# Weights of an MLP moved to another address phase against the moving operand

## The chip, the cores and the metric

The kernel runs on one core of a Trainium2 chip. The metric is the time of one execution on the device in microseconds; lower is better. Each core has a matrix engine (TensorE, PE in the profile, with its weight loads listed apart as PEld), VectorE (DVE), ScalarE (ACT), GpSimd (POOL) and a DMA queue driven by SyncE (SP). Operands lie in SBUF, an on-chip memory of 128 partitions; matrix products are written to PSUM.

A matrix product on TensorE has two operands in SBUF. The weights (128 x 128 here) are loaded into the array by an instruction of their own, and then the moving operand (128 partitions by up to 512 columns) passes through the array.

## The reference

Eight batches of eight heads, 576 positions, head dimension 64. Heads 0 to 3 attend to the last 32 positions, heads 4 to 7 to the positions with the same remainder modulo 32. The attention's output, put back to 512 features a position, goes through a gated MLP with 1,024 hidden features:

```
scores = q @ k.T / 8, masked; attn = softmax(scores); x = attn @ v
h    = maximum(x @ w_in, 0)
conv = conv_w[0]*h[t-1] + conv_w[1]*h[t] + conv_w[2]*h[t+1]
out  = (h * sigmoid(conv)) @ w_out
```

All inputs are 32-bit floats; the kernel gets the weights as pairs of 32-bit words of 64-bit numbers and converts them itself.

## The kernel before, in words

The 4,608 positions are cut into nine groups of 512 (N). For each group the kernel computes four attention steps (one for each pair of heads) of the next batch, the first product of the MLP (`mm1`, L607), the convolution, sigmoid and gate on ScalarE, VectorE and GpSimd (`conv_gate`), and the second product (`mm2`, L672).

Both products are done with split numbers, so that 32-bit accuracy comes out of the faster 32-bit matrix format: every operand is a high part and a low part, and three products are added up: high weights by high moving part, low weights by high moving part, high weights by low moving part. The weights are `wih`, `wil` (first product) and `woh`, `wol` (second); the moving operands are `xh`, `xl` (attention's output, two groups' worth of columns) and `gh`, `gl` (the gated hidden features, one row of 512 columns for each of eight feature blocks; 514 in the last group). Each single matmul has its own weight load of 128 x 128 and, as a rule, 512 moving columns. One block of the first product is 4 x 3 matmuls, one block of the second 8 x 3. The last group's second product is cut into pieces of 256 and 257 columns (258 with the one that is computed twice).

At the beginning the weights are converted (`convert`, L334 to L421): words are loaded into `ws` or `misc`, cut into parts on ScalarE and VectorE, and the low parts are formed by matmuls with the unit matrices `eye`, `eyer` and `negr` (minus one) as weights (L411 to L413, L418, L419).

The order of the instructions on each engine comes from a planner: each operation is entered with an estimated duration and a due time, the planner lays them out, and the program is emitted in that order. The planner knows engines, durations and dependencies; addresses do not enter it.

The tiles in SBUF are allocated from the pools `const` and `mlp`, one after the other in the order in which they are declared, so the order of the declarations sets the addresses. A tile's bytes per partition are the product of its later dimensions and the element size: `xh`, `xl`, `wih`, `wil`, `woh` and `wol` have 16,384 bytes each, `gh` and `gl` 16,448, `diag` 1,280, `eye`, `eyer`, `negr` and `warm` 512, `cwords` 192, `picks` and `small` 128, `cwa` and `cwt` 96, `carry` 64. The declarations stand from L268 on.

Of the kernel before, what the change touches and what calls it, by code (L numbers as in the profile page):

```python
# [10 lines left out]
F32 = _mybir.dt.float32  # L11
F32R = _mybir.dt.float32r
BF16 = _mybir.dt.bfloat16
I32 = _mybir.dt.int32
# [6 lines left out]
P = 128  # L21
W = 32
# [227 lines left out]
def tile_banded_attention_gated_mlp(ctx, tc, qkT, vw, w_in, conv, w_out, masks_in, picks_in, eye_in, out):  # L250
# [3 lines left out]
    D, NSEG, NBLK = 64, 4, 5  # L254
    SEGS = [0, 5, 9, 14, 18]
    NF, NM = w_in.shape[0], w_out.shape[0] // 2
# [11 lines left out]
    const = ctx.enter_context(tc.tile_pool(name="const", bufs=1))  # L268
    xh = const.tile([P, NC, 2 * N], F32R, name="xh")
    xl = const.tile([P, NC, 2 * N], F32R, name="xl")  # L270
    wih = const.tile([P, NC, FF], F32R, name="wih")
    wil = const.tile([P, NC, FF], F32R, name="wil")
    woh = const.tile([P, NF, DM], F32R, name="woh")
    wol = const.tile([P, NF, DM], F32R, name="wol")
    gh = const.tile([P, NF * (N + 2)], F32R, name="gh")
    eye = const.tile([P, P], F32, name="eye")
    eyer = const.tile([P, P], F32R, name="eyer")
    negr = const.tile([P, P], F32R, name="negr")
    picks = const.tile([P, 2, W], BF16, name="picks")
    small = const.tile([P, W], F32, name="small")  # L280
    cwords = const.tile([P, 3 * NF, 2], I32, name="cwords")
    gl = const.tile([P, NF * (N + 2)], F32R, name="gl")

    def attention_buffers(pool, i):
# [10 lines left out]
    mlp = ctx.enter_context(tc.tile_pool(name="mlp", bufs=1))  # L295
# [2 lines left out]
    misc = mlp.tile([P, 2 * NHB * L], F32, name="misc")  # L298
    hs = [misc[:, L * i:L * i + L] for i in range(NHB)]
    cs = [misc[:, L * (NHB + i):L * (NHB + i) + L] for i in range(NHB)]  # L300
    carry = mlp.tile([P, NF, 2], F32, name="carry")
    psum = ctx.enter_context(tc.tile_pool(name="psum", bufs=1, space=PSUM))
    psR = psum.tile([P, 2048], F32, name="r")
    psM = [psum.tile([P, 512], F32, name=f"m{i}") for i in range(NPM)]
# [1 line left out]
    words = [const.tile([P, 8 * P, 2], I32, name=f"ws{i}") for i in range(NWS)]  # L306
    wa = [const.tile([P, 8 * P], I32, name=f"wa{i}") for i in range(NWA)]
    wl = [const.tile([P, 8 * P], F32R, name=f"wl{i}") for i in range(NWL)]
    diag = const.tile([P, 2 * NBLK, W], F32, name="diag")
    cwa = const.tile([P, 3 * NF], I32, name="cwa")  # L310
    cwt = const.tile([P, 3 * NF], I32, name="cwt")

    def slot(n):
        return n % NB
# [368 lines left out]
        if g == NG - 1 and not last:  # L683
            op(Q, 256, at + 6, lambda: nc.sync.dma_start(out=out[ms, first:first + N + 1], in_=o[:, 0:N + 1]), ko, [])

    warm_ = const.tile([P, 256], BF16, name="warm")

    def warm_up():
        nc.vector.memset(warm_, 0.0)
# [113 lines left out]
```

## Time and profile before

| | |
|---|---|
| time, median of 3 runs | 532.12 us (531.75 to 533.3) |
| profiled execution, its own time | 531.87 us |
| its span, first to last instruction | 529.7 us |
| granted TensorE clock, mean | 0.986 |
| busy: TensorE, weight loads, VectorE, ScalarE, GpSimd | 508.4, 409.9, 362.3, 319.8, 118.3 us |
| matmuls of the first product (L607) | 3 x 288 |
| matmuls of the second product (L672) | 3 x 320, of these 3 x 256 with 512 columns |

The profile is of one execution. Matmuls overlap in it: a matmul's listed duration runs from its start to its modelled end, and the next one starts before that, so durations do not add up to the span. Weight loads (PEld) run beside the matmul that stands before them. The granted clock is the share of full speed that TensorE's throttle allowed. "Lnnn" is a line of the kernel.

### The profile page before, as it was taken

What the parts mean: (1) busy time and instruction counts of PE and PEld (TensorE: products, weight loads), DVE (VectorE), ACT (ScalarE), POOL (GpSimd) and SP (SyncE); (2) the same over time, 40 slices, a digit from 0 to 9 for tenths busy, and PEclk for the clock granted to TensorE, in tenths of its full rate; (3) what the DMA queues carried; (4) which work ended last, traced back from release to release, by engine and by line L of the source; (5) the groups of instructions that cost most, each with busy time, mean ns of one, the idle gap of its engine ahead of it and who ended that gap; (6) DMA issues with size and microseconds to landing.
All of it is one profiled execution on the core that took longest, in us unless ns stands there. A gap on an engine that the chain in (4) does not pass through costs nothing.

```text
span 529.7 us, 16633 instructions
## 1 busy us (share of the span) xinstructions
PE 508.4 (96%) x7352; PEld 409.9 (77%) x7352; DVE 362.3 (68%) x639; ACT 319.8 (60%) x492; POOL 118.3 (22%) x197
## 2 busy tenths in 40 slices
PE   4787999999999999999999999999999999999997
PEld 3555677778877887788778877887788788888897
DVE  3977799866785668757975785688658845832940
ACT  2454776856584668656837675577547755733841
POOL 0111201532222112212231222222212221320220
PEclk9797999999999999999999999999999999999999
DMA  8656422352044303520334034303440001001001
GB/s 281 250 189 222 157 78 78 124 178 88 7 136 149 99 1 127 185 76 23 114 107 147 1 124 145 121 0 119 135 134 1 33 11 72 1 16 65 0 36 44
DMA packets 17639, 51.30 MB, mean 97 GB/s; under 512 B 2208, under 2 KB 3360, under 8 KB 17568
## 3 DMA queue, kind: packets, MB, share of 16 engines
q1 hardware_dynamic: 17568, 50.25, 28.1%
q8 instruction: 57, 0.93, 0.7%
q14 instruction: 14, 0.11, 0.1%
HBM read 40.80 MB, written 9.44 MB: 95 GB/s over the span
## 4 chain that ended last, share of the span: by engine, by line
PE 93%; ACT 2%; DVE 2%; DMA 1%; issue 1%; SPq 1%; DVEq 0%; ACTq 0%
PE m L672 39%; PE m L607 37%; PE r L514 6%; PE r L458 4%; PE m L411 2%; PE r L449 1%; DMA misc<-in_dram 1%; PE r L569 1%; PE m L412 0%; PE m L413 0%; ACT xh L549 0%; PE r L486 0%; DVE t L471 0%; DVE mx L470 0%; ACT wa L334 0%
## 5 line engine op out<-in xcount | busy, mean ns | idle before, releaser
L643 DVE SCALAR_TENSOR_TENSOR misc<-misc,cw 128x512 f32<-128x512 f32 (+29 forms) x256 | 126.8, 542 | 35.5 <-ACT misc L634 35.0
L672 PE MATMUL m<-gh,woh 128*128 128x512 f32 (+2 forms) x320 | 123.7, 387 | 0.0
L672 PE MATMUL m<-gh,wol 128*128 128x512 f32 (+2 forms) x320 | 118.2, 370 | 0.0
L672 PE MATMUL m<-gl,woh 128*128 128x512 f32 (+2 forms) x320 | 117.9, 368 | 0.0
L607 PE MATMUL m<-xh,wih 128*128 128x512 f32 x288 | 113.3, 393 | 0.0
L607 PE MATMUL m<-xh,wil 128*128 128x512 f32 x288 | 112.5, 391 | 0.0
L607 PE MATMUL m<-xl,wih 128*128 128x512 f32 x288 | 112.3, 390 | 0.0
L492 POOL TENSOR_TENSOR t<-t,sm 128x640 f32<-128x640 f32 x31 | 45.3, 1462 | 117.6 <-DVE sm L476 82.9
L672 PEld LDWEIGHTS m<-gh,woh 128*128 128x128 f32 x320 | 60.0, 188 | 12.2
L624 ACT ACTIVATE misc<-m 128x512 f32<-128x512 f32 x72 | 42.9, 596 | 42.8 <-PE m L607 41.0
L672 PEld LDWEIGHTS m<-gl,woh 128*128 128x128 f32 x320 | 60.2, 188 | 10.8
L672 PEld LDWEIGHTS m<-gh,wol 128*128 128x128 f32 x320 | 60.2, 188 | 8.4
L607 PEld LDWEIGHTS m<-xh,wih 128*128 128x128 f32 x288 | 54.2, 188 | 11.8 <-issue 0.2
L607 PEld LDWEIGHTS m<-xl,wih 128*128 128x128 f32 x288 | 54.2, 188 | 11.5
L607 PEld LDWEIGHTS m<-xh,wil 128*128 128x128 f32 x288 | 54.2, 188 | 11.0
L648 DVE TENSOR_TENSOR misc<-misc 128x512 f32<-128x512 f32 (+1 forms) x69 | 48.8, 708 | 12.6 <-ACT misc L646 12.4
L634 ACT ACTIVATE misc<-misc,cw 128x512 f32<-128x512 f32 (+1 forms) x70 | 50.5, 724 | 11.1 <-DVE gl L434 4.7
L646 ACT ACTIVATE misc<-misc 128x512 f32<-128x512 f32 (+1 forms) x72 | 44.6, 627 | 14.5 <-DVE misc L643 13.8
L431 ACT CAST gh<-misc 128x512 fp32r<-128x512 f32 (+1 forms) x72 | 44.2, 618 | 14.0 <-DVE misc L648 12.3
L678 ACT COPY misc<-m 128x512 f32<-128x512 f32 (+2 forms) x40 | 21.5, 545 | 47.5 <-PE m L672 47.0
L626 POOL COPY misc<-carry 128x2 f32<-128x2 f32 x64 | 18.9, 295 | 131.2 <-DVE misc L648 95.9
L470 DVE TENSOR_REDUCE mx<-r 128x10 f32<-128x640 f32 x32 | 26.2, 819 | 30.4 <-PE r L458 30.4
(84 smaller groups left out, 584.0 us busy)
## 6 DMA issues: line engine op xcount, KB each, us to landing
qk<-in_dram SPq DMA_DIRECT2D x32, 592.0 KB, 4.0
v<-in_dram SPq DMA_DIRECT2D x32, 384.0 KB, 3.6
ws<-in_dram SPq DMA_DIRECT2D x14, 512.0 KB, 5.1
out_dram<-misc SPq DMA_DIRECT2D x28, 256.0 KB, 3.1
misc<-in_dram SPq DMA_DIRECT2D x2, 512.0 KB, 6.3
out_dram<-misc SPq DMA_DIRECT2D x4, 255.5 KB, 3.4
out_dram<-misc SPq DMA_DIRECT2D x3, 256.5 KB, 2.0
masks<-in_dram SPq DMA_DIRECT2D x2, 160.0 KB, 2.6
```

Source lines behind the costliest of these rows:

```text
L431: op(A, ta, at, lambda: nc.scalar.copy(hi(), src), [skey], [(k, "h") for k in [key] + over])
L470: op(V, 0.826, at + offset[0], lambda: nc.vector.tensor_reduce(out=mx, in_=p3, axis=AX.X, op=ALU.max), ks, [("mx", i)])
L492: op(G, 1.28, at + offset[5], lambda: nc.gpsimd.tensor_tensor(out=t, in0=t, in1=sm.unsqueeze(2).to_broadcast([P, 2 * NBLK, 64]), op=ALU.mu ...
L514: nc.tensor.matmul(psV[64 * h:64 * h + 64, o:o + n_], v[W * c:W * c + W, h, j], tt[W * c:W * c + W, 64 * NBLK * h + a:64 * NBLK * h + z], ...
L607: nc.tensor.matmul(ps, a[:, c, fs], x[:, c, N * x0:N * x0 + N], start=(n == 0 and m == 0), stop=(n == NC - 1 and m == 2))
L624: op(A, 0.596, at + cg[2], lambda: nc.scalar.activation(out=h[:, 2:N + 2], in_=ps, func=AF.Relu), [kp], [("h", hi)])
L634: op(A, 0.725, at + cg[3], lambda: nc.scalar.activation(out=c_[:, :n], in_=h[:, 1:n + 1], func=AF.Copy, scale=w1), kh + ["cw"], [kc] + new)
L643: op(V, 0.11 + 0.00117 * (z - a), at + cg[4] + 0.4 * k, lambda k=k, wk=wk, a=a, z=z: nc.vector.scalar_tensor_tensor(out=c_[:, a:z], in0=h[ ...
L646: op(A, 0.63, at + cg[5], lambda: nc.scalar.activation(out=c_[:, :n], in_=c_[:, :n], func=AF.Sigmoid), [kc], [kc], table=1)
L648: op(ge, 0.69 if ge == V else 1.28, at + cg[6], lambda: (nc.vector if ge == V else nc.gpsimd).tensor_tensor(out=c_[:, :n], in0=h[:, 1:n + ...
L672: nc.tensor.matmul(ps, a[:, f, ms], row(y, g, f)[:, tok], start=(f == 0 and n == 0), stop=(f == NF - 1 and n == 2))
L678: op(A, 0.59 if z - a0 == N else 0.38, at + 3 * t + 3, lambda ps=ps, a0=a0, z=z: nc.scalar.copy(o[:, a0:z], ps), [("M", mi)], ko)
```

## The change

Only the order of declarations changes. `cwords` moves ahead of the weights; `diag`, `eye` and `carry` come to stand between the weights and `gh`; `warm`, `cwa` and `cwt` come to stand between `gh` and `gl`. `carry` moves from the pool `mlp` to `const`. No operation, dependency or due time is touched.

```diff
     xh = const.tile([P, NC, 2 * N], F32R, name="xh")
     xl = const.tile([P, NC, 2 * N], F32R, name="xl")
+    cwords = const.tile([P, 3 * NF, 2], I32, name="cwords")
     wih = const.tile([P, NC, FF], F32R, name="wih")
     wil = const.tile([P, NC, FF], F32R, name="wil")
     woh = const.tile([P, NF, DM], F32R, name="woh")
     wol = const.tile([P, NF, DM], F32R, name="wol")
+    diag = const.tile([P, 2 * NBLK, W], F32, name="diag")
+    eye = const.tile([P, P], F32, name="eye")
+    carry = const.tile([P, NF, 2], F32, name="carry")
     gh = const.tile([P, NF * (N + 2)], F32R, name="gh")
-    eye = const.tile([P, P], F32, name="eye")
     eyer = const.tile([P, P], F32R, name="eyer")
     negr = const.tile([P, P], F32R, name="negr")
     picks = const.tile([P, 2, W], BF16, name="picks")
     small = const.tile([P, W], F32, name="small")
-    cwords = const.tile([P, 3 * NF, 2], I32, name="cwords")
+    warm_ = const.tile([P, 256], BF16, name="warm")
+    cwa = const.tile([P, 3 * NF], I32, name="cwa")
+    cwt = const.tile([P, 3 * NF], I32, name="cwt")
     gl = const.tile([P, NF * (N + 2)], F32R, name="gl")
...
-    carry = mlp.tile([P, NF, 2], F32, name="carry")
...
-    diag = const.tile([P, 2 * NBLK, W], F32, name="diag")
-    cwa = const.tile([P, 3 * NF], I32, name="cwa")
-    cwt = const.tile([P, 3 * NF], I32, name="cwt")
...
-    warm_ = const.tile([P, 256], BF16, name="warm")
```

## The prediction

> **What bounds the kernel now.** I read the page first: busy time, the slices, the chain of waits by line, then the costliest groups.
>
> ```profile
> span 529.7 us, 16633 instructions
> PE 508.4 (96%) x7352; PEld 409.9 (77%) x7352; DVE 362.3 (68%) x639; ACT 319.8 (60%) x492; POOL 118.3 (22%) x197
> ...
> PEclk9797999999999999999999999999999999999999
> ...
> PE 93%; ACT 2%; DVE 2%; DMA 1%; issue 1%; SPq 1%; DVEq 0%; ACTq 0%
> PE m L672 39%; PE m L607 37%; PE r L514 6%; PE r L458 4%; PE m L411 2%; PE r L449 1%; DMA misc<-in_dram 1%; PE r L569 1%; PE m L412 0%; PE m L413 0%; ACT xh L549 0%; PE r L486 0%; DVE t L471 0%; DVE mx L470 0%; ACT wa L334 0%
> ```
>
> TensorE is busy for 96% of the span and makes 93% of the chain; the two MLP products, L607 (first) and L672 (second), make 76% of the chain. No other engine is above 68%. The view by stretches says where TensorE is not the bound:
>
> ```profile
> core 0: us, PE busy (x) PEld busy (x) DVE busy (x) ACT busy (x) POOL busy (x), PEclk, DMA share, GB/s
> 0.00:50.00 50.00, 33.26 (x898) 24.68 (x898) 34.73 (x55) 20.85 (x27) 6.84 (x12) 0.87 0.68 239
> ...
> 85.00:480.00 395.00, 395.00 (x5873) 318.23 (x5872) 275.55 (x516) 252.50 (x391) 100.33 (x171) 1.00 0.26 87
> ```
>
> Only in the first 50 us does TensorE idle much (33.26 of 50). From 85 to 480 us it never stops, at a granted clock of 1.00, while VectorE is busy for 275.55 of 395 us, 70%. So from 85 us on the time is the sum of TensorE's start-to-start distances, and I read those next. "Busy" for one matmul (390 ns) is longer than its distance to the next, since matmuls overlap; the distance is what counts. The chain of waits in order of time (start, length, what) gives it from long unbroken runs:
>
> ```profile
> 280.58 21.80 PE m L607 x96
> ...
> 336.11 13.19 PE m L607 x57
> ...
> 462.46 19.04 PE m L672 x84
> 481.50 21.76 PE m L607 x96
> 503.26 22.89 PE m L672 x192
> ```
>
> 21.76 / 96 = **226.7 ns** for each matmul of 128x512 in the first product; 19.04 / 84 = 226.7 in the second. The run at 336 us comes right after an attention step: 13.19 / 57 = 231.4. The last group is cut into 256 and 258 columns (257 in the mean): 22.89 / 192 = 119.2.
>
> What would it be without any hindrance? At half clock the trace has the answer:
>
> ```profile
> 49.35:51.06 1.71, 1.71 (x5) 0.50 0.50 196
> ```
> ```profile
> 50.63 0.61 PE L413 MATMUL m<-wih,negr 128*128 128x512 f32 x1
> 51.06 1.08 PE L411 MATMUL m<-ws,eye 128*128 128x512 f32 x2
> ```
>
> At clock 0.50 a 512-column matmul is followed by the next after 0.43 us, so the columns themselves take about 0.43 / 2 = 0.215 us at full clock, with the rounding of these starts 0.21 to 0.22. A second row is the short bf16 warm-up at full clock, whose length grows with each matmul that the window lets in:
>
> ```profile
> 32.11 0.34 PE L523 MATMUL r<-warm 128*128 128x192 bf16 x2
> ...
> 32.11 0.42 PE L523 MATMUL r<-warm 128*128 128x192 bf16 x3
> ...
> 32.11 0.50 PE L523 MATMUL r<-warm 128*128 128x192 bf16 x4
> ```
>
> 0.08 us for 192 columns is 0.417 ns a column; 512 such columns are 213.3 ns. So every f32 matmul of the MLP takes **13.4 ns more** than its columns. What runs beside it is the next weight load:
>
> ```profile
> 336.38 0.40 PE L607 MATMUL m<-xh,wil 128*128 128x512 f32 x1
> 336.62 0.40 PE L607 MATMUL m<-xl,wih 128*128 128x512 f32 x1
> 336.86 0.40 PE L607 MATMUL m<-xh,wih 128*128 128x512 f32 x1
> 337.09 0.40 PE L607 MATMUL m<-xh,wil 128*128 128x512 f32 x1
> 337.32 0.39 PE L607 MATMUL m<-xl,wih 128*128 128x512 f32 x1
> 337.55 0.39 PE L607 MATMUL m<-xh,wih 128*128 128x512 f32 x1
> 337.78 0.40 PE L607 MATMUL m<-xh,wil 128*128 128x512 f32 x1
> 338.02 0.39 PE L607 MATMUL m<-xl,wih 128*128 128x512 f32 x1
> ```
> ```profile
> 336.38 0.19 PEld L607 LDWEIGHTS m<-xl,wih 128*128 128x128 f32 x1
> 336.62 0.19 PEld L607 LDWEIGHTS m<-xh,wih 128*128 128x128 f32 x1
> ```
>
> Each load starts with the matmul ahead of its own (336.38 and 336.38). After the interruption the distances are 0.24, 0.24, 0.23, 0.23, 0.23, 0.23, 0.24 us and settle at 226.7 later. The same instructions on the same addresses thus take different times: the surplus is not one fixed step of the instruction. It fits two reads of SBUF, moving operand and weights, that get in each other's way depending on how they lie in time. That is my reading, not a thing the trace names.
>
> **The change, part by part.** No instruction, wait or DMA is added, removed or moved: the planner's costs hold no address. What moves is addresses. In bytes per partition, modulo 512, measured from xh: before, xh, xl and the four weight tiles are 16,384 each, so all start at 0, and so does gh; gh's surplus of 64 and picks, small and cwords (128 + 128 + 192) make 512, so gl is at 0 too. A weight block is 128 f32, 512 bytes, and a moving row of the first eight groups 2,048. After, cwords (192) lies ahead of the weights: they start at 192. diag, eye and carry (1,280 + 512 + 64) fill up to 2,048, so gh is at 0, and eyer, negr, picks, small, warm, cwa and cwt (1,984) with gh's 64 bring gl to 0 again. So the change is one thing: the weights' phase against the moving operand goes from 0 to 192.
>
> How many matmuls feel it: L607 864, L672 768 of 512 columns (the groups list them), together **1,632**, and the last group's 192 halves.
>
> ```profile
> L607 PE MATMUL m<-xh,wih 128*128 128x512 f32 x288 | 113.3, 393 | 0.0
> L607 PE MATMUL m<-xh,wil 128*128 128x512 f32 x288 | 112.5, 391 | 0.0
> L607 PE MATMUL m<-xl,wih 128*128 128x512 f32 x288 | 112.3, 390 | 0.0
> L672 PE MATMUL m<-gh,woh 128*128 128x512 f32 x256 | 105.7, 413 | 0.0
> ```
>
> The phase's price at 192 is shown nowhere in the trace, so I bound it. Best: the surplus goes, 226.7 to 213.3 ns, 1,632 x 13.4 = 21.9 us. Worst: the matmuls never settle and stay at the mean after an interruption, 231.4: 1,632 x 4.7 = 7.7 us lost. The surplus changes with small shifts in time, and a shift of addresses shifts the same two reads against each other, so I hold a change of the surplus likelier than none. I take **half of it away**, 6.7 ns: there is no row that is nearer to one end, since the settled 226.7 lies inside the range that the rows show and nothing shows a complete escape. Of the 1,632 the first group's 96 run between 47 and 82 us among weight conversions, on loads that TensorE waits for; I count them at nothing (0.6 us if that cover is gone). 1,536 x 6.7 = **10.3 us**.
>
> The last group has a floor of its own. Weight loads alone, in the trace's low-part matmuls of 2 to 144 columns, follow each other thus:
>
> ```profile
> 42.44 0.86 PEld L569 LDWEIGHTS r<-xh,negr 128*128 128x128 f32 x7 [0.85 <-ACT xh L549]
> ```
>
> (0.86 - 0.19) / 6 = 0.112 us, so 119.2 can fall to 112 at most: 192 x 7.2 = 1.4 us; I take half, **0.7 us**, bounds 0 to 1.4.
>
> The rest has one answer, nothing: eye as weights now at 448 instead of 64 (24 matmuls of L411, 10 ns each is 0.2 us either way), diag used once, warm, cwa, cwt and carry read by engines that are not the bound; attention's tiles move by 2,048, phase unchanged; the f32 tiles of ScalarE and VectorE in misc by 64, hidden under TensorE's 395 of 395 us. Without that cover the whole would cost what those engines lose, and they have 119 us of slack there.
>
> Sum: 10.3 + 0.7 = 11.0 us. The profiled execution took 531.87 (span 529.7 and 2.2 around it), so 520.9; the median of the runs is 0.25 above it, so **521 us**.
>
> The Trainium skill, TensorE: Matmul & The Clock Gate (section "Wait — 56ns, not 53.3ns?"), gives warm back-to-back matmuls N / 2.4 GHz plus about 2.5 ns, 215.7 at 512 columns. The trace's 226.7 is not that. By the page's figure as the floor, the best case would be 1,632 x 11.0, about 18 us (an estimate from that page).
>
> **The rivals.** *Nothing changes* (532). Moving operand and weights don't meet in SBUF, or they meet as often at each phase: the load reads 512 bytes while the moving operand passes more than that, so every phase may be crossed. For it speak the matmuls of the weight conversion, where the phase is already another (eyer and negr at 64, the moving wl at 288):
>
> ```profile
> 79.73 0.40 PE L418 MATMUL m<-wl,eyer 128*128 128x512 f32 x1
> 79.97 0.39 PE L419 MATMUL m<-woh,negr 128*128 128x512 f32 x1
> 80.20 0.40 PE L418 MATMUL m<-wl,eyer 128*128 128x512 f32 x1
> 80.43 0.39 PE L419 MATMUL m<-woh,negr 128*128 128x512 f32 x1
> 80.66 0.39 PE L607 MATMUL m<-xh,wih 128*128 128x512 f32 x1
> ```
>
> Their distances are 0.24, 0.23, 0.23, 0.23: no phase among these escapes. And in the last group the rows of gh and gl lie 8 bytes further with each block, yet the mean stays. Against it: four matmuls never settle, the last group is near its load floor, and 192 is not among these phases.
>
> The same page of the Trainium skill (section "Step-by-step: what each phase is for") states this rival's rule: TensorE has two independent read ports, and loading the next weights takes no bandwidth from the running matmul. By it the time stays at 532. The unsteady distances above speak against it here, the four rows at other phases for it.
>
> *Slower*: at phase 192 the stream settles late or not at all, and the distance stays at that of the run after an interruption, 231.4. Place: all L607 and L672 runs. Price: 1,632 x 4.7 = 7.7 us, 532.1 + 7.7 = **540**. It decides from a settled distance of 227.7, where 1,632 x 1 ns passes 1.6 us. For it: the settled value of phase 0 is already lower than the mean after interruptions, so another phase could lose it. Against: it would have to hold everywhere.
>
> *Faster, but given back*: TensorE runs ahead and waits for VectorE in attention steps. At 70% busy it could; if half the gain went there, 526.5. I keep it inside the forecast's own range.
>
> **How the numbers follow.** Forecast (surplus cut): chance 0.50, own range 510 (all of 21.9 and 1.4 us would be 509) to 530. Nothing changes: 0.28. Slower: 0.22, 534 to 540. About 0.3%, 1.6 us, is what a measurement of this kernel can tell from no change. The range that holds 8 in 10 leaves out the slower rival's far half: 510 to 538. Faster 0.50, same 0.28, slower 0.22.
>
> **What would show it.** In the changed profile the run of 96 matmuls of L607 near 480 us should take 21.1 us (220 each) and the 192 halves 22.2. If the 96 take 21.76 again, nothing changed; 22.2 or more is the slower rival. If the runs shorten and the span doesn't, TensorE's idle time between 85 and 480 us, now none, shows what gave it back. Instruction counts and the granted clock must stay. I am wrong in the main step if the distance after the change is outside 213 to 226.

## The result and the profile after

The changed kernel takes **534.85 us** (median of 6 runs, 534.55 to 535.81); the kernel before took 531.9 (6 runs, 530.82 to 533.3). The ratio is 1.0058, with a 95% interval of 1.0041 to 1.0074: slower by 0.6%, where 521 us had been forecast.

The page of the changed kernel, with the lines that answer to those of before (each line number is one higher):

```profile
span 532.4 us, 16633 instructions
PE 511.8 (96%) x7352; PEld 410.7 (77%) x7352; DVE 362.5 (68%) x639; ACT 319.8 (60%) x492; POOL 119.3 (22%) x197
...
PEclk9997999999999999999999999999999999999999
...
PE 93%; DMA 2%; ACT 2%; DVE 1%; issue 1%; SPq 1%; ACTq 0%
```

Instruction counts are the same on each engine, VectorE and ScalarE are busy as long as before (362.5 and 319.8 us, GpSimd 1 us longer), and TensorE still makes 93% of the chain. TensorE's busy time has grown by 3.4 us, the span by 2.7. The view by stretches, cut at the same places of the program, for the kernel before and then for the changed one (length, TensorE busy, loads busy, VectorE, ScalarE, GpSimd, clock, DMA):

```profile
121.22:503.26 382.04, 382.04 (x5126) 308.98 (x5126) 262.28 (x491) 241.44 (x376) 90.85 (x162) 1.00 0.23 76
```
```profile
121.39:505.81 384.42, 384.42 (x5126) 309.13 (x5126) 262.53 (x491) 241.48 (x376) 91.90 (x162) 1.00 0.23 76
```

2.38 of the 2.7 us arise in this stretch, in which TensorE never idles and which holds the same 5,126 matmuls; the start gives 0.17 (its first 50 us at a granted clock of 0.94, where the kernel before had 0.87), the last group 0.15. The long runs in the chain of waits (start, length, what):

```profile
281.55 21.98 PE m L608 x96
337.48 13.27 PE m L608 x57
...
464.61 19.23 PE m L673 x84
483.83 21.97 PE m L608 x96
505.81 22.99 PE m L673 x192
```

21.97 / 96 = **228.9 ns** where it was 226.7 (21.76 / 96), and 19.23 / 84 = 228.9 in the second product. From the starts of all matmuls in the two traces one sees which ones lost. (An interruption is any other work on TensorE between two of these matmuls, mostly an attention step; there are 61 runs without one.) The first distance of a run is long, 334 ns in the mean before and 338 after. The second to the eleventh have nearly the same mean in both kernels (567 of them: 230.4 ns before, 230.1 after). Those from the twelfth on (942) have 226.67 before, nearly all 226 or 227, and 228.89 after, where most go round a cycle of 232, 226 and 229. 942 x 2.2 = 2.1 us, most of the 2.7; the rest isn't traced further. Before, a run settles: from some matmul on its distances stay at 226 or 227 ns to its end. After, it goes round the dearer cycle instead.

### The profile page after: what moved, and what is told of

Its sections match the earlier page's. It is cut to its first block, busy times and chain, and to the rows that moved or that the text cites. A ratio compares the mean times of both kernels' runs of the same rounds, so it can differ in the third digit from the quotient of the medians.

```text
span 532.4 us, 16633 instructions
## 1 busy us (share of the span) xinstructions
PE 511.8 (96%) x7352; PEld 410.7 (77%) x7352; DVE 362.5 (68%) x639; ACT 319.8 (60%) x492; POOL 119.3 (22%) x197
## 4 chain that ended last, share of the span: by engine, by line
PE 93%; DMA 2%; ACT 2%; DVE 1%; issue 1%; SPq 1%; ACTq 0%
PE m L673 39%; PE m L608 37%; PE r L515 6%; PE r L459 4%; PE m L412 2%; PE r L450 1%; DMA misc<-in_dram 1%; DMA ws<-in_dram 1%; ACT wa L335 1%; PE m L413 1%; PE m L414 1%; PE r L487 0%; PE r L570 0%; ACT xh L550 0%; DVE t L472 0%
```

## Experiments

Two words are kept apart here. The *offset* is how many bytes the weights lie behind the moving operand, modulo 512: 0 before, 192 in the changed kernel (the expectations call it phase or distance too). The *distance*, in ns, is the time from one matmul's start to the next. In most of the kernels the offset is set by padding tiles between the operands, and the number to read is the distance in a long run: the 96 matmuls of the first product near 485 us, and the 84 of the second ahead of them. The fences show rows of each kernel's chain of waits in order of time (start, length, what, how many). The diffs are cut: where one shows a line of the first product alone, the second has the same edit, and a pad that only brings the tiles behind it back to their places may be left out. Unless an interval is given, a time is that of one execution beside one of the kernel before on the same chip, and rougher than these runs.

### Is it the offset, or the weights' own address?

Everything shifted by 192, offset 0:

```diff
+    const.tile([P, 48], F32, name="pad1")
     xh = const.tile([P, NC, 2 * N], F32R, name="xh")
```

> Every tile lies 192 bytes further, so that the weights sit on the addresses (modulo 512) of the changed kernel, but xh, xl, gh and gl move with them and the distance between the two is 0 as before. Theory P (only the distance of weights to moving operand modulo 512 counts): the settled distance of two matmuls stays at 226.7 ns, the run of 96 at 21.76 us, time 532. Rival A (the weights' own address modulo 512 counts): 228.9 ns, 21.97 us, time 535.

```profile
463.84 19.04 PE m L673 x84
482.88 21.76 PE m L608 x96
```

226.7 ns in both products; 533.25 us beside 533.91. Then the reverse: the weights stay, the moving operands move by 320.

```diff
+    const.tile([P, 80], F32, name="pad1")
     xh = const.tile([P, NC, 2 * N], F32R, name="xh")
     xl = const.tile([P, NC, 2 * N], F32R, name="xl")
+    const.tile([P, 48], F32, name="pad2")
     wih = const.tile([P, NC, FF], F32R, name="wih")
...
+    const.tile([P, 80], F32, name="pad3")
     gh = const.tile([P, NF * (N + 2)], F32R, name="gh")
...
+    const.tile([P, 48], F32, name="pad4")
```

> The weights stay on their addresses modulo 512 of the kernel before; xh, xl, gh and gl move by 320 instead, so that the weights lie 192 behind them. Theory P: settled distance 228.9 ns, the run of 96 21.97 us, time 535. Rival A: 226.7 ns, 532. If something else that moved in the change did it (eye, diag, carry, misc), this is 226.7 too.

```profile
465.34 19.23 PE m L676 x84
484.56 21.97 PE m L611 x96
```

228.9, 535.24 us beside 533.91. The offset counts, not the weights' own address, and the small tiles that the change put in other places aren't needed for the loss: here they keep their order.

Only the first product's weights at 192:

```diff
+    const.tile([P, 48], F32, name="pad1")
     wih = const.tile([P, NC, FF], F32R, name="wih")
     wil = const.tile([P, NC, FF], F32R, name="wil")
+    const.tile([P, 80], F32, name="pad2")
     woh = const.tile([P, NF, DM], F32R, name="woh")
```

> Only the first product's weights lie at 192, those of the second at 0. Theory P: long runs of the first product 228.9 ns a matmul, long runs of the second 226.7; time about 533.5, half of the change's loss. If the loss came from one shared state of the engine, both products would show one value.

```profile
463.54 19.04 PE m L674 x84
482.58 21.98 PE m L609 x96
```

The first product loses, the second doesn't (533.17 beside 533.91, too small a difference for single executions). Each product's offset acts on its own runs.

### Other offsets

The same kind of pads, with the weights of both products at 256, 64, 128, 224 and 32 behind the moving operand; only the two lengths change. For 16 the tiles of all four weights are made longer and read from word 4 on (counted from 0):

```diff
+    const.tile([P, 64], F32, name="pad1")
     wih = const.tile([P, NC, FF], F32R, name="wih")
...
+    const.tile([P, 64], F32, name="pad2")
     gh = const.tile([P, NF * (N + 2)], F32R, name="gh")
```
```diff
-    wih = const.tile([P, NC, FF], F32R, name="wih")
+    wih = const.tile([P, NC * FF + 128], F32R, name="wih")[:, 4:4 + NC * FF].rearrange("p (c n) -> p c n", c=NC)
```

> Weights of both products at 256 behind the moving operand. Theory P gives no value for 256; if 0 is the one place where the stream settles, 228.9 or more and 535 or more; if the settled distance goes up and down with the phase, it can lie below 226.7 too, down to 213.3 (510 us).

```profile
462.86 19.04 PE m L674 x84
481.90 21.76 PE m L609 x96
```

> Weights of both products 64 behind the moving operand. So far 0 and 256 settle at 226.7 ns, 192 runs in a cycle with a mean of 228.9. If the period is 128 bytes, 64 is 228.9 (535); if 192 is one bad place in a period of 256, 64 is open and may be 226.7.

```profile
128.53 13.50 PE m L609 x57
...
476.04 19.60 PE m L674 x84
495.64 22.40 PE m L609 x96
```

> Weights of both products 128 behind. Period 128: 226.7 ns, 532. Period 256: open, any value from 213.3 to 231.

```profile
470.54 19.52 PE m L674 x84
490.06 22.31 PE m L609 x96
```

> Weights of both products 224 behind the moving operand. Settled distances so far: 0: 226.7, 64: 233.3, 128: 232.5, 192: 228.9, 256: 226.7. If the curve falls evenly from 192 to 256, 224 is between 226.7 and 228.9, time 532 to 535. If the best place lies beside 256, it is below 226.7 and the kernel faster than before.

```profile
122.96 13.50 PE m L609 x57
...
470.40 19.60 PE m L674 x84
490.00 22.40 PE m L609 x96
```

> Weights 32 behind. By the curve so far between 226.7 (0) and 233.3 (64): about 230, 537. If 0 only holds because the stream settles there, 32 may settle too, at 226.7.

```profile
470.91 19.60 PE m L674 x84
490.51 22.40 PE m L609 x96
```

> Weights 16 behind. If the settled state forgives small shifts, 226.7 and 532. If the curve has no flat part, one quarter of the way from 0 to 64: about 228.3, 534.5.

```profile
283.30 21.76 PE m L607 x96
...
465.93 19.60 PE m L672 x84
485.53 22.40 PE m L607 x96
```

| offset of the weights, bytes | 0 | 16 | 32 | 64 | 128 | 192 | 224 | 256 |
|---|---|---|---|---|---|---|---|---|
| mean distance in the run of 96, ns | 226.7 | 226.7 or 233.3 | 233.3 | 233.3 | 232.4 | 228.9 | 233.3 | 226.7 |
| one execution, us | | 536.58 | 541.5 | 546.68 | 541.11 | | 541.01 | 532.3 |

The kernels before on the same chips took 532.39 to 533.91. Offset 0 was already the best of these, with 256, and the change went to the next best. 32 and 224 cost 1.7% and 1.6% of the time. The 546.68 us at 64 hold more than the offset's price: the distances are those of 224, but the run of 57 starts at 128.53 us where at 224 it starts at 122.96, behind a start with a lower granted clock (0.83 in the first 50 us, 0.89 at 224). From there to the end of the span the two take the same, 416.0 and 415.9 us; the kernel before takes 408.5.

At 16 one and the same program runs 96 matmuls at 226.7 ns (at 283 us) and later, on the same addresses, at 22.40 / 96 = 233.3 (at 485 us). Each run that is long enough to show it keeps the state in which it settled to its end; the last one, 309 matmuls over both products, stays at 233.3. So the offset alone doesn't fix a price; it decides which repeating states a run can fall into. That what comes before picks one is my reading; which part of it does, these runs don't show. In units of one column, 0.417 ns, 226.7 is 512 + 32 columns and 233.3 is 512 + 48. Two expectations missed: 224 isn't between 192 and 256 but worse than both, and 32 isn't between 0 and 64 but as dear as 64.

Two more kernels for the period and for the width of the good place. First product at 448 and second at 320:

```diff
+    const.tile([P, 112], F32, name="pad1")
     wih = const.tile([P, NC, FF], F32R, name="wih")
     wil = const.tile([P, NC, FF], F32R, name="wil")
+    const.tile([P, 96], F32, name="pad2")
     woh = const.tile([P, NF, DM], F32R, name="woh")
```

> First product's weights at 448 (192 more than 256), second product's at 320 (64 more than 256). If the phase counts modulo 256: long runs of the first product 228.9 ns with the changed kernel's cycle (232, 226, 229), of the second 233.3 as at 64. If it counts modulo 512, both are open and at least one is off these values.

```profile
467.67 19.59 PE m L675 x84
487.26 21.99 PE m L610 x96
```

First product 8 bytes behind, second 8 bytes ahead (tiles read from word 2 and, with 504 = -8, from word 126 on):

```diff
+    wih = const.tile([P, NC * FF + 128], F32R, name="wih")[:, 2:2 + NC * FF].rearrange("p (c n) -> p c n", c=NC)
...
+    woh = const.tile([P, NF * DM + 128], F32R, name="woh")[:, 126:126 + NF * DM].rearrange("p (c n) -> p c n", c=NF)
```

> First product's weights 8 bytes behind the moving operand, second product's 8 bytes ahead. 16 behind settled in two ways, some runs at 226.7 and some at 233.3. If 0 lies in the middle of a small basin, both products settle at 226.7 here in most runs; if the basin ends at 0 on one side (224, which is 32 ahead, gave 233.3), the second product is above 226.7. A value below 226.7 would be a better place than before.

```profile
468.97 19.60 PE m L672 x84
488.57 22.14 PE m L607 x96
```

448 behaves as 192 (229.1, and in the later part of the run the same cycle of 232, 226, 229), 320 as 64 (233.2), 256 as 0: the offset counts modulo 256 in these three pairs. The good place is narrow: 8 bytes behind and 8 bytes ahead, each tried in one product, lose it (230.6 and 233.3), although 16 reaches it in some runs.

### What the surplus is made of

The moving operand stands still: each matmul reads its first column 512 times. Then the same with the weights at 64.

```diff
-  nc.tensor.matmul(ps, a[:, c, fs], x[:, c, N * x0:N * x0 + N], ...
+  nc.tensor.matmul(ps, a[:, c, fs], x[:, c, N * x0:N * x0 + 1].to_broadcast([P, N]), ...
-  nc.tensor.matmul(ps, a[:, f, ms], row(y, g, f)[:, tok], ...
+  nc.tensor.matmul(ps, a[:, f, ms], row(y, g, f)[:, tok][:, 0:1].to_broadcast([P, tok.stop - tok.start]), ...
```

> The addresses of the kernel before, but the moving operand of both products reads its first column again and again (step 0), so the products are not the reference's. Theory C (the surplus of 13.4 ns is two sweeping reads that meet in SBUF): the moving read stands on one place and the distance falls towards 213 to 217 ns, some 16 to 22 us less. Rival F (a fixed price of each f32 matmul with its weight load, whatever is read): 226.7 stays.

```profile
446.02 18.20 PE m L672 x84
464.22 20.80 PE m L607 x96
485.02 21.49 PE m L672 x192
```

> Weights 64 behind, where the settled distance was 233.3 ns, and the moving operand reads its first column again and again (step 0), so the products are not the reference's. Theory C (phase and surplus are one thing, the sweeping moving read against the weight read): 215 to 218 ns here too, about 512 us, as at phase 0. Rival (the phase has a price of its own, whatever the moving read does): the 6.6 ns between 226.7 and 233.3 stay, about 223 ns and 523 us.

```profile
445.27 18.20 PE m L674 x84
463.47 20.80 PE m L609 x96
484.27 21.49 PE m L674 x192
```

20.80 / 96 = 216.7 ns in both, 512.13 and 511.36 us beside 533.28 and 533.21. Of the surplus of 13.4 ns 10 go away, and so does the whole difference between the offsets 0 and 64: both need a moving read that walks through SBUF, as they would if they were one thing. Also the last group's halves fall to 21.49 / 192 = 111.9, the spacing of weight loads.

The weights stand still instead (one column read 128 times):

```diff
-  nc.tensor.matmul(ps, a[:, c, fs], x[...
+  nc.tensor.matmul(ps, a[:, c, f * P:f * P + 1].to_broadcast([P, P]), x[...
```

> The addresses of the kernel before, but every weight load reads one column 128 times (step 0), so the products are not the reference's. Theory C: the weights' read stands on one place, the moving read passes it, distance 213 to 220 ns. Rival F: 226.7.

```profile
468.01 19.46 PE m L672 x84
487.47 22.24 PE m L607 x96
```

22.24 / 96 = 231.7 ns, 537.96 us beside 533.28: slower, not faster. Theory C's second half fell: the weights need not walk for the surplus to be there.

Is the surplus paid for each weight column? First the middle product with 64 columns, then all but the first and last matmul of a chain with 68:

```diff
-  nc.tensor.matmul(ps, a[:, c, fs], x[...
+  nc.tensor.matmul(ps if m != 1 else ps[:64], a[:, c, fs] if m != 1 else a[:, c, f * P:f * P + 64], x[...
```
```diff
+  all_ = (n == 0 and m == 0) or (n == NC - 1 and m == 2)
-  nc.tensor.matmul(ps, a[:, c, fs], x[...
+  nc.tensor.matmul(ps if all_ else ps[:68], a[:, c, fs] if all_ else a[:, c, f * P:f * P + 68], x[...
```

> The addresses of the kernel before; of the three products the middle one (low weights by high moving part) loads and uses only 64 of 128 weight columns, so half of that product is left out. Theory C: the load beside the matmul before it is half as long, meets the moving read half as often, and the distance of that matmul falls by about half of the surplus, to some 220 ns; a group of three takes 673 instead of 680, and the time falls by about 3.6 us. Rival F (a price for each load, not for each column): 680 ns and 532.

```profile
464.76 19.31 PE m L672 x84
484.06 22.05 PE m L607 x96
```

> Phase 0 as before, but of each chain of 12 (24) matmuls only the first and the last load 128 weight columns; the others load and use 68, so that part of the products is left out. Theory L (the surplus grows with the length of the weight load beside it): the loads are 0.53 as long, the surplus falls from 13.4 to some 7 to 8 ns, distance about 221, some 9 us less. Rival S (what counts is in which repeating state the two reads settle, not how long the load is): 226.7 to 233, no time won, 530 to 545.

```profile
459.72 19.04 PE m L674 x84
478.76 21.76 PE m L608 x96
```

With 64 columns in one of three the stream no longer settles (229.7, 534.62 us beside 532.39), with 68 in nearly all the long runs settle at just 226.7. A load half as long has the same surplus: not a price for each column. What the second kernel gains (528.95 beside 533.28, spans 526.8 and 531.1) lies for the most part elsewhere: the first distance after an interruption is 334 ns in the mean before and 291 with the short loads, 61 x 43 = 2.6 of 4.3 us. There the second matmul's load isn't fetched ahead. In most runs it starts 107 ns behind the first matmul before, and 56 ns with the short loads; the second matmul follows this load by about 230 ns in both. So the first distance falls by what the load starts earlier.

High weights at offset 0, low weights at 128 (first product) and at 64 (second):

```diff
     wih = const.tile([P, NC, FF], F32R, name="wih")
+    const.tile([P, 32], F32, name="pad1")
     wil = const.tile([P, NC, FF], F32R, name="wil")
+    const.tile([P, 96], F32, name="pad2")
     woh = const.tile([P, NF, DM], F32R, name="woh")
+    const.tile([P, 16], F32, name="pad3")
     wol = const.tile([P, NF, DM], F32R, name="wol")
+    const.tile([P, 112], F32, name="pad4")
     gh = const.tile([P, NF * (N + 2)], F32R, name="gh")
```

> High weights at 0, low weights at 128 in the first product and at 64 in the second, so that one load in three has another phase than the others. If each matmul pays the price of the load beside it, the means are (2 x 226.7 + 232.5) / 3 = 228.6 and (2 x 226.7 + 233.3) / 3 = 228.9. If one load of another phase breaks the settled state, 230 or more. If the three phases can help each other, below 226.7.

```profile
467.50 19.42 PE m L676 x84
486.92 22.20 PE m L611 x96
```

231.3 and 231.2 ns, above the weighted means of 228.6 and 228.9: one load of three at another offset takes the settled state from the whole stream.

Last, the direction: the moving operand is read from its last column to its first and the result written backward.

```diff
-  nc.tensor.matmul(ps, a[:, c, fs], x[:, c, N * x0:N * x0 + N], ...
+  nc.tensor.matmul(ps[:, ::-1], a[:, c, fs], x[:, c, N * x0:N * x0 + N][:, ::-1], ...
```

> The addresses of the kernel before; the moving operand of both products is read from its last column to its first, and the result is written in the same backward order, so the output is the reference's. The surplus goes where the moving read stands still, so the way that read sweeps past the weights should matter. Theory C (two reads that sweep past each other): another distance than 226.7; below it, if the meeting gets shorter, and then faster than both kernels. If direction plays no part: some value of the same set, 226.7 to 233.3, 532 to 546.

```profile
470.43 19.60 PE m L672 x84
490.03 22.40 PE m L607 x96
```

Here the stream does settle, each distance 233 or 234 ns, but in the dearer state: 541.56 us, 1.0177 of the kernel before (interval 1.0124 to 1.023). A backward read starts at another address and passes the weights in another way, and the result is written backward too; this run can't say which of them did it.

None of these kernels that compute the reference's output is faster than the kernel before by more than single executions differ.

## Why the prediction was wrong, point by point

**What bounds the kernel** was right: TensorE's distances set the time from 85 us on, VectorE and ScalarE were busy as long as before, and the changed distances account for most of the loss. The shape of the sum (a number of matmuls by a difference of distances) holds.

**The surplus as two reads that meet** was right in part. It was read from distances that vary on the same addresses, and the standing moving read takes most of it away. The Trainium skill's rule in TensorE: Matmul & The Clock Gate (section "Step-by-step: what each phase is for"), that a weight load takes no bandwidth from the running matmul, would have the distances alike; here 226.7 to 233.3 by offset alone disagrees. What I had not seen is that neither a shorter load nor one that stands still lowers the distance (226.7 and 231.7).

**The failed step** is "half of it away": 1,536 matmuls at 220 ns instead of 226.7, 10.3 us won. Measured were 228.9 ns, 2.1 us lost. I held a lower surplus likelier than a higher one and took the middle between 226.7 and 213.3, although no row spoke for the lower side. The rows that did speak lay in the same prediction: after an interruption the distances are 0.24, 0.24 and 0.23 us and come down to 226.7 later. The settled value was thus already below what the stream takes before it settles, and a change of the offset could lose that; no row showed a lower value that it could win. The mechanism was wrong with it: I took the surplus for a price that shifts with the offset, where the runs show a few repeating states, and at offset 0 the cheapest of those tried. Of eight offsets, none is below 226.7.

**The range** of 510 to 538 holds the measured 534.85 us, but by the half of the slower rival that it took in and not by the forecast's mechanism. Of the signs named in advance, the distance of 228.9 lies outside 213 to 226, the sign of a wrong main step; the run of 96, 21.98 us, lies between the sign of no change (21.76) and that of the slower rival (22.2 or more), which had been set by that rival's price.

**The slower rival** named the mechanism, a stream that settles late or not at all, and was given 0.22. Its price was too high in both factors. It charged 1,632 matmuls, but about 690 of them stand among the first dozen of their run, where both kernels have nearly the same mean; the 942 behind them lost. And it charged 4.7 ns from a misread row: the run of 57 with its 231.4 isn't unsettled throughout. It starts with a distance of 341 ns, settles after eleven and runs at 226.7 from there on. The cycle at offset 192 has 228.9: 942 x 2.2 = 2.1 us in place of 7.7.

**The rival "nothing changes"** leaned on the conversion's matmuls at other offsets, 0.23 to 0.24 us. They are four in a row behind other work, and in the kernel before a run can take up to eleven distances to settle, so these rows couldn't tell. That objection stood beside them, and was right.

**The last group**: forecast 0.7 us less, measured 22.99 instead of 22.89. Its floor of 112 ns was right, as the standing moving read shows (111.9), but the change doesn't lead there.

**The rest at nothing** is not contradicted: moving the operands apart without the new order of declarations gives the changed kernel's long runs (21.97 and 19.23 us). The part of the small tiles was not measured by itself, and the two profiled starts, where `eye` is used, ran at different clocks.

## What to carry to other kernels

Where identical matmuls stand in a long row, take their start-to-start distance, and look at it apart for the first dozen after an interruption and for the rest: if the rest is lower and constant, the stream has settled, and a change of the operands' relative addresses can lose that. Measure a few offsets before moving operands; here 0 and 256 were best, and 32 bytes cost 1.7%. A surplus that one can see is not a gain that one can have: ask which row shows the lower value.

## What the runs showed of the hardware

- In long runs the distance between the starts of two 128x512 matmuls on 32-bit operands, each with its own weight load, depends on how many bytes the weights lie behind the moving operand: 226.7 ns at 0 and 256, 228.9 at 192, 232.4 at 128, 233.3 at 32, 64 and 224; 448 and 320 behave as 192 and 64.
- One program can hold two states on the same addresses: at 16 bytes 226.7 ns in some runs and 233.3 in others, each kept to the run's end.
- With a moving operand that stands on one column the distance is 216.7 at 0 and at 64. A weight read that stands on one column has 231.7, a load of 68 columns instead of 128 the same 226.7.
- At offset 0 a run settles after at most eleven distances (2, 5, 10 or 11 in the 25 runs that are long enough to show it). The first distance is 334 ns in the mean, the second to the eleventh 230.4.
- The first distance depends on the weight load: with loads of 68 columns in most matmuls instead of 128 it is 291 ns.
- Open: whether the two reads share something in SBUF, and what, and why the steps are 32 and 48 columns. The runs show when the price is paid, not what charges it.
